# One attention, Fourier and FFN kernel: a list scheduler's order of operations replaced by a written one

## The chip, the cores and the metric

The kernel runs on one core of one Trainium2 chip. The metric is the device time of one execution in microseconds (us). Engines are named as the profile names them: PE (TensorE), PEld (its weight loads), DVE (VectorE), ACT (ScalarE), POOL (GpSimd), SP (SyncE, which issues most DMAs). PE is in order, as every engine is: an instruction that waits holds up all behind it on its engine.

## The reference

Sliding-window attention of 8 batches, 8 heads, 576 tokens and 64 columns a head, then the real part of a two-dimensional Fourier transform added to the input, a normalisation over the 512 columns, and a two-layer FFN with 2048 hidden columns:

```python
    mask = (rel >= 0) & (rel < window)          # window = 64
    scores = np.where(mask, scale * q @ k^T, -1e9)
    attn = np.exp(scores - max); attn = attn / (sum + 1e-09)
    x = (attn @ v), heads side by side           # 8 x 576 x 512
    X = np.fft.fft(np.fft.fft(x, axis=1), axis=2)
    u = x + np.real(X)
    un = (u - mu) / np.sqrt(var + 1e-06)
    out = u + np.maximum(un @ w_ch1, 0.0) @ w_ch2
```

## The kernel before

The 4608 tokens are 36 attention tiles of 128 rows (the code's T). Tiles 0 to 10 ("whole") work in f32 and are turned on PE; the others ("split") carry each number as a high and a low f16 half and are turned by transposing DMAs. For each tile: q and k are loaded, turned (flips, line 539; copies of the results, kst and qbd, by the helper `copy`, line 474 on ACT, 478 on DVE or GpSimd), multiplied (scores, 659 or 668 and 673), masked and exponentiated (ACT, 705), turned (722 on PE for whole tiles; for split ones the low half is a subtraction, `p_lo`, 736, and the turn a DMA, `p_turn`, 741), and multiplied with v (775). `v_own` (618) copies half a tile of v to the place from which the next tile reads it.

Eight Fourier stages, one a batch, follow the tiles (a radix-4 step on DVE at 810, its turn at 884 to 899, matmuls at 1035 to 1139). `norm_tile` gathers the mixed rows with an indirect DMA (GpSimd, 1246), takes the statistics (1261), scales (1295, un), and turns the result (1307, pu) into the operand of the FFN, uhl. The FFN works on 18 chunks of 256 tokens. Chunk 0 is in f32; chunks 1 to 10 use three f16 products (first layer 1507, ph; relu 1519 and 1522, hh; second layer 1487, po); chunks 11 to 17 use a seven-product scheme (`ffn7`: sums of operands at 1827, products px and py at 1755 and q at 1863, results gathered at 1896 to 1906, sent out at 1942 and 1945). The weights come in 32 pieces, which DVE converts (1394 to 1406) and ACT squares for their scale (1412).

All 3568 operations are first recorded: `op(eng, dur, prio, fn, reads, writes, ...)` keeps an engine, an assumed duration, a priority and, for 'alt' operations, a second engine that could do the same. Buffers are rings; a DMA, PE, DVE, ACT or POOL operation can take a slot once one is free. `Plan.order()` (278) then builds the program by a list scheduler: at each step it takes, among the ready operations, the one that can start first, with ties by priority; an operation that two engines can do goes to the one that would end sooner by a margin. Priorities come from formulas and from the tables NUDGE, LEAD and BIAS. DVE's operations that hold the port shared with GpSimd and GpSimd's own are assumed to exclude each other in time. The final loop (2021) emits the operations in that order; where the assumed gap on PE ahead of one is above 0.8 us, it puts in warm matmuls (1997), fillers that compute nothing, one for each 0.21 us beyond 0.4, in the early part only.

Of the kernel before, what the change touches and what calls it, by code (L numbers as in the profile page):

```python
# [67 lines left out]
NUDGE = {  # L68
    "": {0: 14.4, 1: 16.6, 2: -0.4, 3: 15.9, 4: 69.4, 5: 25.3, 6: -12, 8: 0.2, 10: 3.8, 11: -27.5},
    "even": {14: -0.3},  # L70
    "ffn7": {16: -0.6, 232: 0.3, 1276: 3.2, 2005: 0.6, 2006: 0.7, 2047: 12.4, 2100: -0.7, 2120: 1.3, 2141: -0.3, 2145: -0.1, 2146: 0.5, 2167: 0.2},
    "first": {21: 0.8, 32: -0.1, 62: 1.2},
    "odd": {34: -2.9},
    "piece": {0: 10.6},
    "split": {3: -0.1, 25: -0.2},
}
LEAD = {
    "": (
        0,
    ),  # L80
    "even": (
        0, 0, 0, 0, 0, 0, 0, 0,
    ),
    "ffn7": (
        0, 0, 0, 0, 0, 0, 0, 0, 0, 0, 0, 0, 0, 0, 0, 0,
        0, 0,
    ),
    "norm": (
        0, 0, 0, 0, 0, 0, 0, 0, 0, 0.4, 0, 0, 0, 0, 2.6, 2.6,
        3.9, 3.9, 3.9, 4, 3.9, 4.1, 3.9, 3.9, 3.9, 3.9, 3.9, 3.9, 3.9, 3.9, 3.9, 3.9,  # L90
        3.9, 3.9, 3.9, 3.9,
    ),
    "part": (
        0.3, 0.3, 0.3, 0.3, 0.3, 0.3, 0.3, 0.3, 0.3, 0.3, 0.3, 0.3, 0.3, 0.3, 0.3, 0.3,
        0.3, 0.3, 0.3, 0.3, -1.7, 0.3, 0.3, 0.3, 0.3, 0.3, 0.3, 0.3, 0.3, 0.3, 0.3, 0.3,
    ),
    "piece": (
        0, 0, 0, 0, 0, 0, 0, 0, 0, 0, 0, 0, 0, 0, 0, 0,
        0, 0, 0, 0, 0, 0, 0, 0, 0, 0.1, 0, 0.8, 0.8, 0.8, -9.9, -9.9,
    ),  # L100
    "pre1": (
        0, 0, 0, 0,
    ),
    "prep": (
        0, 0, 0, 0,
    ),
    "scale": (
        0, 0,
    ),
    "tail": (  # L110
        0, 0, 0, 0, 0, 0, 0, 0, 0, 0, 0, 0,
    ),
    "whole": (
        0, 0, 0, 0, -1.5, -1.5, -1.5, -1.5, -2.9, -2.9, -2.9, -2.9, -2.9, -2.9, -2.9, -2.9,
        -2.9, -2.9, -2.9, -2.9, -4.6, -2.9, -2.9, -2.9, -2.9, -2.9, -2.9, -2.9, -2.9, -2.9, -2.9, -2.9,
        -2.9, -2.9, -3.1, -3.1,
    ),
}
BIAS = {
    "ffn7": {21: -0.4},  # L120
    "first": {13: -0.8},
}
# [80 lines left out]
class Plan:  # L203
# [74 lines left out]
    def order(self):  # L278
# [5 lines left out]
        for o in self.ops:  # L284
            o.wait, o.ready = len(o.deps), 0.0
            for d in o.deps:
                d.outs.append(o)
# [1741 lines left out]
```

## Time and profile before

| | us |
|---|---|
| median of 3 runs (lowest, highest) | 946.46 (944.35, 946.49) |
| the profiled execution, its own time | 946.62 |
| its span | 944.8 |
| PE busy | 928.9 (98%) |
| DVE busy | 800.1 (85%) |
| ACT busy | 594.5 (63%) |
| POOL busy | 313.6 (33%) |

The span is the time between the first and the last instruction that the profile shows; 1.8 us lie outside it. Idle time of an engine that does not bound the kernel costs nothing by itself. What matters is where PE, busy 98% of the span, stands still, and what it waits for there.

### The profile page before, as it was taken

The numbers are of one execution on the slowest core, as the hardware profiler recorded it, in microseconds if no ns is written. First come the engines' busy times: TensorE is split into PE (matmuls) and PEld (weight loads), VectorE is DVE, ScalarE is ACT, GpSimd is POOL, SyncE is SP. The second block draws the span as 40 slices with busy tenths as digits, with TensorE's granted clock in tenths as the row PEclk, the third lists the DMA queues.
The fourth block names the chain that finished last, engine by engine and source line by source line (L and its number), as shares of the span: only waits on it lengthen the run. The fifth ranks groups of instructions, "written<-read, shape, count | busy, mean of one in ns | idle before, by whom it ended". The sixth has DMA issues, their size and how long they took to land.

```text
span 944.8 us, 25747 instructions
## 1 busy us (share of the span) xinstructions
PE 928.9 (98%) x10193; PEld 720.3 (76%) x10193; DVE 800.1 (85%) x1922; ACT 594.5 (63%) x1545; POOL 313.6 (33%) x348
## 2 busy tenths in 40 slices
PE   8999999999999999999999999999999999999997
PEld 6776767666676676677676667676788999999997
DVE  4989988888898798897788999799988788887776
ACT  6866587787686576878686675445346554655432
POOL 1111031242444453554342254313012255554120
PEclk9999999999999999999999999999999999999999
DMA  9979963279999999999999863513111343232000
GB/s 190 304 184 260 272 131 99 63 156 188 205 211 202 194 182 214 201 198 222 178 202 202 159 142 88 134 28 81 42 45 57 63 96 76 44 85 47 18 25 24
DMA packets 313257, 130.23 MB, mean 138 GB/s; under 512 B 291624, under 2 KB 292264, under 8 KB 313136
## 3 DMA queue, kind: packets, MB, share of 16 engines
q1 hardware_dynamic: 310272, 119.53, 59.1%
q0 software_dynamic: 2720, 8.92, 3.6%
q8 instruction: 80, 1.31, 0.6%
q14 instruction: 41, 0.34, 0.1%
q10 hardware_dynamic: 144, 0.13, 0.0%
HBM read 62.85 MB, written 22.04 MB: 90 GB/s over the span
## 4 chain that ended last, share of the span: by engine, by line
PE 75%; DVE 10%; DMA 6%; issue 5%; ACT 3%; POOL 1%; SPq 1%; POOLq 0%; ACTq 0%; DVEq 0%
PE ph L1507 19%; PE po L1487 19%; PE q L1863 11%; PE py L1755 5%; PE ph L1728 4%; PE px L1755 4%; PE pa L775 3%; PE pg L1043 2%; DMA pt<-flex 2%; PE psc L659 2%; PE pz L1095 2%; DMA mt<-md,gix 1%; DVE y L810 1%; PE pp L722 1%; ACT pr L705 1%
## 5 line engine op out<-in xcount | busy, mean ns | idle before, releaser
L1507 PE MATMUL ph<-uhl,w0s 128*128 128x256 f16 (+1 forms) x2040 | 262.1, 279 | 2.3 <-DVE hh L1522 1.3
L1487 PE MATMUL po<-w1s,hh 128*128 128x512 f16 (+1 forms) x1024 | 263.3, 393 | 0.6 <-DVE hh L1522 0.3
L1507 PEld LDWEIGHTS <-w0s 128*128 128x128 f16 x1920 | 185.6, 98 | 50.1 <-issue 3.0
L1487 PEld LDWEIGHTS <-hh 128*128 128x128 f16 x960 | 91.4, 98 | 82.3 <-DVE hh L1522 1.6
L1519 ACT ACTIVATE hh<-ph 128x512 f16<-128x512 f32 x80 | 47.3, 592 | 56.3 <-PE ph L1507 50.9
L705 ACT ACTIVATE pr<-pr,nm 128x128 f32<-128x128 f32 x200 | 77.5, 391 | 1.9 <-DVE nm L694 1.8
L1246 POOL DMA_INDIRECT mt<-md,gix x34 | 42.8, 1259 | 87.4 <-DVE xu L1261 39.8
L1863 PEld LDWEIGHTS <-qbd 128*128 128x128 f16 x672 | 64.9, 98 | 7.6 <-DVE qbd L1827 0.5
L1522 DVE SCALAR_TENSOR_TENSOR hh<-ph,hh 128x512 f16<-128x512 f32 x80 | 54.7, 684 | 16.3 <-ACT hh L1519 15.8
L1863 PEld LDWEIGHTS <-kst 128*128 128x128 f16 x504 | 49.3, 98 | 5.7
L478 POOL COPY yp<-y 128x1024 uint16<-128x1024 uint16 x24 | 28.7, 1195 | 73.4 <-DVE y L810 52.2
L1827 DVE TENSOR_TENSOR flex<-flex 128x256 f32<-128x256 f32 x91 | 40.2, 442 | 14.8 <-ACT flex L1822 6.0
L694 DVE CUSTOM_DVE_ANT_0 pr<-psc,mskb 128x128 f32<-128x128 f32 x200 | 45.5, 282 | 0.6 <-PE psc L659 0.5
L1755 PEld LDWEIGHTS <-wa 128*128 128x128 f16 x750 | 45.6, 98 | 0.2
L1755 PEld LDWEIGHTS <-w0s 128*128 128x128 f16 x720 | 44.9, 98 | 0.2
L1798 ACT ACTIVATE flex<-flex 128x384 f32<-128x384 f32 x40 | 20.7, 518 | 37.2 <-DVE flex L1778 37.1
L1840 ACT CAST qbd<-flex 128x1024 f16<-128x1024 f32 x28 | 29.2, 1042 | 23.7 <-DVE flex L1827 12.9
L1728 PE MATMUL ph<-uhl,w0s 128*128 128x256 f16 x384 | 43.5, 273 | 0.0
L474 ACT COPY qbd<-qbd 64x1024 uint16<-64x1024 uint16 x40 | 41.7, 1043 | 2.7 <-DMA qbd<-flex 1.7
L478 POOL COPY yT<-py 128x1024 uint16<-128x1024 uint16 (+2 forms) x24 | 26.5, 1107 | 47.7 <-DMA py<-yp 45.0
L1863 PE MATMUL q<-w1s,qbd 128*128 128x256 f16 x336 | 41.4, 273 | 0.2 <-DVE qbd L1827 0.2
L1728 PEld LDWEIGHTS <-w0s 128*128 128x128 f16 x384 | 37.6, 98 | 5.2
(285 smaller groups left out, 2132.9 us busy)
## 6 DMA issues: line engine op xcount, KB each, us to landing
wd<-in_moe_w_ch SPq DMA_DIRECT2D x26, 512.0 KB, 5.5
out<-xu SPq DMA_DIRECT2D x34, 256.0 KB, 2.8
kn<-in_k SPq DMA_DIRECT2D x32, 256.0 KB, 3.4
qn<-in_q SPq DMA_DIRECT2D x32, 256.0 KB, 4.5
xd<-xa SPq DMA_DIRECT2D x30, 256.0 KB, 3.1
xu<-xd SPq DMA_DIRECT2D x30, 256.0 KB, 3.5
flex<-in_v SPq DMA_DIRECT2D x22, 256.0 KB, 3.8
md<-mp SPq DMA_DIRECT2D x24, 192.0 KB, 3.5
```

The costliest lines, as they stand in the source:

```text
L474: nc.scalar.mul(out, in_, scale) if scale is not None else nc.scalar.copy(out, in_)
L478: eng.tensor_copy(out, in_)
L694: nc.vector.tensor_tensor_reduce(out=t["pr", jj][:, hp], in0=t["ps", jj][:, hp], in1=mskb[:, m : m + P], scale=-0.125, scalar=3.0e38, op0= ...
L705: nc.scalar.activation(pr, src, AF.Exp, bias=t["nm", jj][:, hp : hp + 1], scale=-1.0, accum_out=t["rc"][:, hp, jj])
L1246: nc.gpsimd.indirect_dma_start(out=mts[T], out_offset=None, in_=mds[pb][0 : HR if n < 4 else 2 * HR], in_offset=bass.IndirectOffsetOnAxis( ...
L1487: nc.tensor.matmul(t["po"][i], l_, r_, start=(f == 0 and x == 0), stop=(f == NKF - 1 and x == len(mm) - 1))
L1507: nc.tensor.matmul(ph, l_, r_, start=(x == 0), stop=(x == len(mm) - 1))
L1519: nc.scalar.activation(t["hh", pr][:, 0], ph, AF.Relu)
L1522: nc.vector.scalar_tensor_tensor(out=hh[:, 1], in0=ph, scalar=0.0, in1=hh[:, 0], op0=ALU.max, op1=ALU.subtract)
L1728: nc.tensor.matmul(ph, l_, r_, start=(x == 0), stop=(x == len(mm) - 1))
L1755: nc.tensor.matmul(to[:, x], l_(a, k_), r_(b_, k_), start=(y == 0), stop=(y == 5))
L1863: nc.tensor.matmul(t["q"][q_][:, y], l_[:, a, i, m], r_(b_, m), start=(s_ + y + m + x == 0), stop=(s_ == 3 and m == 1 and x == 2 and (y == ...
```

## The change

The list scheduler is gone. A tuple ORDER of 3568 numbers holds the order of all operations on all engines: a number n at or above 0 is operation n on its first engine, and -1 - n is operation n on its second. `Plan.follow(ORDER)` walks it, sets engine and place, and works out assumed starts only to find the gaps on PE in which warm matmuls go. The tables NUDGE, LEAD and BIAS are removed. The operations, their arithmetic and their buffers' rings are the same; code behind the tables stands 30 lines lower. The tuple was made by a search with a price on the waits of GpSimd for the shared port, over five sets of assumed durations.

```diff
-NUDGE = {
-    "": {0: 14.4, 1: 16.6, 2: -0.4, 3: 15.9, 4: 69.4, 5: 25.3, 6: -12, 8: 0.2, 10: 3.8, 11: -27.5},
...
+ORDER = (
+    2, 3, 0, 1, 174, 178, 179, 173, 176, 177, 4, 181, 186, 196, 182, 199, 197, 201, -203, 200, 204, 183, 184, 187,
...
-    def order(self):
+    def follow(self, order):
...
+        for n in order:
+            o = self.ops[max(n, -1 - n)]
+            o.eng = list(o.durs)[n < 0]
+            o.dur, o.ready = o.durs[o.eng], 0.0
+            for d in o.deps:
+                late = self.LATE[d.eng] * (o.slack if "PE" in o.durs else 0.0 if d.eng in o.durs else o.wary)
+                o.ready = max(o.ready, d.free + (self.SEM if d.eng not in o.durs or d.lat else self.SELF)[d.eng] + late)
+            locks = o.lock if o.eng == "POOL" else o.eng == "DVE" and o.port
+            st = max(free[o.eng], o.ready, port if locks else 0.0)
+            for b in o.allocs:
+                st = max(st, slots[b.ring].pop(0))
+            gap, o.st = st - free[o.eng], st
...
-        for o, gap in zip(plan.order(), plan.gaps):
+        for o, gap in plan.follow(ORDER):
```

Operations on each engine, before and after: PE 726 and 726, DVE 1265 and 1231, ACT 847 and 807, POOL 262 and 336, DMAs 468 and 468. Warm matmuls: 49 and 32. Three places follow, as the built program has them, in the engine's order; names are those of tiles with a running number, and x4 is four alike.

PE ahead of the first bank (ph) of the FFN's chunk 0: turns of probabilities (pp), of k and q (pk, pq) and of the normalised tiles (pu). Before:

```order
L539 MATMUL pk_1154<-ident,kn_1111 128x128 x4
L1307 MATMUL pu_1165<-ident,un_1085 128x128 x4
L1997 LDWEIGHTS ident
L1997 MATMUL warm<-ident 128x256
...
L722 MATMUL pp_0_1178<-ident,flex 128x128 x4
L1307 MATMUL pu_1187<-ident,un_1113 128x128 x4
L722 MATMUL pp_1_1195<-ident,flex 128x128 x4
L539 MATMUL pq_1202<-ident,qn_1134 128x128 x4
L1507 MATMUL ph_0_1211<-uhl_1166,w0s 128x256 x4
```

The same place on PE after, up to the masks of a later tile's scores (psc):

```order
L1169 MATMUL pm_1026<-mp_0_983,put 128x512
L569 MATMUL pq_1067<-ident,qn_943 128x128 x4
L752 MATMUL pp_0_1075<-ident,flex 128x128 x4
L569 MATMUL pq_1081<-ident,qn_963 128x128 x4
L1337 MATMUL pu_1098<-ident,un_1096 128x128 x4
L752 MATMUL pp_0_1112<-ident,pr_0_821 128x128 x4
L698 LDWEIGHTS ident
L698 MATMUL psc_0_1121<-mskb,ident 128x512
```

Of the turns ahead of chunk 0, the first pu now stands between a pq and a pp, with the scores (psc) of a later tile behind, and the warm matmuls between them are gone.

ACT ahead of the second copy of uhl (the operand of chunk 0). Before:

```order
L1412 ACTIVATE junk_6_1024,ssq_86<-w0s 128x512
L474 COPY v_81<-v_82 64x1024
L474 COPY kst<-pk_1053 128x512
L474 ACTIVATE qbd_78<-pq_1068 128x512
L474 COPY kst<-pk_1080 128x512
L474 COPY yT_910<-py_1129 128x4x128
L705 ACTIVATE flex,rc_1145<-psc_0_1089,nm_0_1124 128x128 x4
L705 ACTIVATE flex,rc_1145<-psc_1_1091,nm_1_1141 128x128 x4
L474 COPY uhl_1166<-pu_1165 128x4x128
L474 COPY flex<-pp_0_1178 128x512
L474 COPY uhl_1166<-pu_1187 128x4x128
```

The same place on ACT after:

```order
L1442 ACTIVATE junk_3_1030,ssq_87<-w1s 128x512
L1442 ACTIVATE junk_7_1032,ssq_86<-w0s 128x512
L735 ACTIVATE flex,rc_1036<-psc_0_994,nm_0_1034 128x128 x4
L504 COPY pt_1_1042<-pp_1_1041 128x512
L735 ACTIVATE flex,rc_1036<-psc_1_996,nm_1_1060 128x128 x4
L504 COPY kst<-pk_1053 128x512
L504 ACTIVATE qbd_78<-pq_1067 128x512
L504 COPY flex<-pp_0_1075 128x512
L504 ACTIVATE qbd_77<-pq_1081 128x512
L504 COPY uhl_1099<-pu_1098 128x4x128
L504 COPY pt_0_1113<-pp_0_1112 128x512
L504 COPY uhl_1099<-pu_1146 128x4x128
```

The copy of v and one copy of yT that stood here are gone from ACT; copies of pt, kst and qbd stand ahead of the uhl copies.

GpSimd at the end of its list: sums of operands and low halves (1827, in the new file 1857) and the additions of results (1896, now 1926). Before:

```order
L1205 TENSOR_TENSOR up_3_13890<-t_17_13663,up_3_13890 128x256
L1827 TENSOR_TENSOR flex<-flex 128x256
L1827 TENSOR_TENSOR kst<-flex,kst 128x768
L1827 TENSOR_TENSOR flex<-flex 128x256 x4
L1896 TENSOR_TENSOR xu_12625<-xu_12625,flex 128x256
L1827 TENSOR_TENSOR qbd_77<-flex,qbd_77 128x1024
L1827 TENSOR_TENSOR flex<-flex 128x256
L1896 TENSOR_TENSOR xu_13364<-xu_13364,flex 128x256 x2
```

The end of GpSimd's list after:

```order
L1926 TENSOR_TENSOR xu_12648<-xu_12648,flex 128x256
L1926 TENSOR_TENSOR xu_12884<-xu_12884,flex 128x256 x2
L1857 TENSOR_TENSOR kst<-flex,kst 128x768
L1857 TENSOR_TENSOR flex<-flex 128x256 x2
L1857 TENSOR_TENSOR kst<-flex,kst 128x768
L1857 TENSOR_TENSOR flex<-flex 128x256 x2
L1857 TENSOR_TENSOR qbd_77<-flex,qbd_77 128x1024
L1857 TENSOR_TENSOR kst<-flex,kst 128x768
L1857 TENSOR_TENSOR flex<-flex 128x256
L1926 TENSOR_TENSOR xu_13333<-xu_13333,flex 128x256 x2
```

More low halves of kst stand on GpSimd now in the last chunk (three, before one), ahead of the same two final additions.

## Rows read from the trace of the kernel before

**Rows 1.** Stretches: us, then PE, PEld, DVE, ACT, POOL busy, PEclk, DMA, GB/s

```profile
0.00:6.00 6.00, 3.91 (x19) 2.79 (x20) 0.00 (x0) 1.28 (x1) 2.66 (x12) 1.00 0.69 155
6.00:42.00 36.00, 34.69 (x502) 28.40 (x501) 27.17 (x52) 27.82 (x100) 3.10 (x4) 1.00 0.95 253
42.00:47.00 5.00, 3.89 (x54) 2.86 (x52) 4.81 (x12) 4.73 (x24) 1.53 (x1) 1.00 0.93 316
47.00:73.00 26.00, 25.88 (x236) 18.88 (x235) 22.92 (x54) 15.72 (x58) 3.95 (x6) 1.00 0.77 194
73.00:84.00 11.00, 9.09 (x89) 6.69 (x88) 10.62 (x25) 8.07 (x27) 2.03 (x2) 1.00 0.97 229
...
100.00:675.00 575.00, 570.51 (x5927) 403.51 (x5926) 502.79 (x1295) 393.26 (x1030) 210.85 (x226) 1.00 0.79 161
675.00:940.00 265.00, 264.77 (x3235) 245.60 (x3232) 215.99 (x459) 133.33 (x277) 87.29 (x96) 1.00 0.22 52
...
sum 945.00, PE 928.91 PEld 720.27 DVE 800.09 ACT 594.51 POOL 313.62; mean PE 103.21 PEld 80.03 DVE 88.90 ACT 66.06 POOL 34.85
```

**Rows 2.** The same for the warm matmuls alone, 0 to 100 us

```profile
73.00:84.00 11.00, 1.75 (x10) 1.00 0.97 229
...
sum 100.00, PE 9.34; mean PE 1.56
```

**Rows 3.** Chain that ended last, 67 to 84 us: start, length, what

```profile
74.99 0.46 DVE un L1295
...
78.89 1.97 ACT flex L705 x11
```

**Rows 4.** PE timeline, 71 to 84: start, length, what, idle before

```profile
79.51 0.66 PE L1307 MATMUL pu<-ident,un 128*128 128x128 f32 x4 [0.75 <-ACT flex L705]
...
81.40 0.64 PE L1307 MATMUL pu<-ident,un 128*128 128x128 f32 x4
...
83.22 1.25 PE L1507 MATMUL ph<-uhl,w0s 128*128 128x256 f32 x5
```

**Rows 5.** ACT by line and form, 0 to 84: busy, mean ns, idle

```profile
L474 ACT COPY v<-v 64x1024 uint16<-64x1024 uint16 x5 | 5.2, 1043 | 2.5 <-issue 2.5
...
L474 ACT COPY pt<-pp 128x512 f32<-128x512 f32 x6 | 3.6, 612 | 3.3 <-PE pp L722 3.3
```

**Rows 6.** Waits of PE, 100 to 675 us: total, times, longest

```profile
PE pa L775 <- DMA pt<-flex: 0.9, 2, 0.6
```

**Rows 7.** Timeline of PE around attention tile 21

```profile
350.24 0.64 PE L659 MATMUL psc<-kst,qbd 128*64 128x128 f16 x16
...
361.65 1.47 PE L1507 MATMUL ph<-uhl,w0s 128*128 128x256 f16 x12
362.96 1.46 PE L1487 MATMUL po<-w1s,hh 128*128 128x512 f16 x6
...
367.50 0.85 PE L775 MATMUL pa<-v,pt 128*64 128x64 f16 x42 [0.26 <-DMA pt<-flex]
```

**Rows 8.** Timeline of SP's DMA queue, 359 to 366 us

```profile
361.00 4.17 SPq L741 DMA_TRANSPOSE pt<-flex  x2
```

**Rows 9.** Line 741, transposes of probabilities, 330 to 690: min/median/max

```profile
L741 SPq DMA_TRANSPOSE pt<-flex x34: 1231/1288/2818, 333.3 to 593.6; - x34
...
DMA to landing us min/median/max: 3.1/4.8/6.6
```

**Rows 10.** Groups of POOL and of DVE by line and form, whole span

```profile
L736 POOL TENSOR_TENSOR flex<-pr,flex 128x512 f16<-128x512 f32 x20 | 26.8, 1342 | 24.4 <-ACT flex L474 19.0 <-DVE flex L478 5.0 <-DMA pt<-flex 0.4
...
L736 DVE TENSOR_TENSOR flex<-pr,flex 128x512 f16<-128x512 f32 x30 | 21.4, 715 | 0.7 <-ACT flex L474 0.4
```

**Rows 11.** Timelines of PE, POOL and DVE, end of the span

```profile
939.35 0.82 PE L1863 MATMUL q<-v,qbd 128*128 128x256 f16 x6
...
939.78 1.41 POOL L1896 TENSOR_TENSOR xu<-xu,flex 128x256 f32<-128x256 f32 x2 [24.58 <-DVE flex L1906]
...
941.22 0.48 DVE L1898 SCALAR_TENSOR_TENSOR xu<-q,osc,xu 128x256 f32<-128x256 f32 x1 [0.20 <-POOL xu L1896]
```

More of the change, by code (lines that the diff above doesn't have):

```diff
@@ L67 @@
 C_AT = ("fh", "fh", "pt", "pt")
-NUDGE = {
-    "": {0: 14.4, 1: 16.6, 2: -0.4, 3: 15.9, 4: 69.4, 5: 25.3, 6: -12, 8: 0.2, 10: 3.8, 11: -27.5},
[L70 to L122, printed above, removed]
+ORDER = (
[149 rows of a table added]
+)
 VS = 64.0
@@ L199 @@
 class Op:
-    __slots__ = ("eng", "dur", "lat", "fn", "deps", "outs", "prio", "wait", "ready", "allocs", "bufs", "idx", "durs", "margin", "port", "slack", "wary", "group", "lock")
+    __slots__ = ("eng", "dur", "lat", "fn", "deps", "outs", "prio", "wait", "ready", "allocs", "bufs", "idx", "durs", "margin", "port", "slack", "wary", "group", "lock", "free", "st")
 class Plan:
@@ L217, in __init__ @@
     def __init__(self, rings, fifo):
[L218 removed]
+        self.rings, self.fifo, self.ops = dict(rings), fifo, []
         self.slack = self.wary = 0.0
@@ L276, in pe_time @@
         return t
[L278 removed]
+    def follow(self, order):
         busy = {}
[L280 to L282 removed]
+        free = {e: 0.0 for o in self.ops for e in o.durs}
         slots = {r: [0.0] * n for r, n in self.rings.items()}
[L284 to L287, printed above, removed]
[L288 to L298 removed]
@@ L352, in order @@
             free[o.eng] = end
-            if o.lock if o.eng == "POOL" else o.eng == "DVE" and o.port:
+            if locks:
                 port = end
-            done = end + o.lat
-            for b in o.allocs:
-                s_ = sorted(slots[b.ring])
-                slots[b.ring] = s_[1:]
-                if b.ring in line:
-                    line[b.ring].pop()
+            o.free = end + o.lat
             for b in o.bufs:
                 b.left -= 1
-                b.free_at = max(b.free_at, done + self.SEM[o.eng])
+                b.free_at = max(b.free_at, o.free + self.SEM[o.eng])
                 if b.ring and b.left == 0:
                     slots[b.ring].append(b.free_at)
-            for x in o.outs:
-                x.wait -= 1
-                late = self.LATE[o.eng] * (x.slack if "PE" in x.durs else 0.0 if o.eng in x.durs else x.wary)
-                x.ready = max(x.ready, done + (self.SEM if o.eng not in x.durs or o.lat else self.SELF)[o.eng] + late)
-                if not x.wait:
-                    for e in x.durs:
-                        avail[e].append(x)
-            res.append((st, o))
+            res.append((o, gap))
         self.span = max(free.values())
-        self.times = [st for st, _ in res]
-        return [o for _, o in res]
+        return res
 @with_exitstack
```

65 lines of the change are left out of this document (1 added, 64 removed), and 148 rows, old and new, of the table ORDER.

## The prediction

> **What bounds the kernel now.** I read the busy time of each engine over the whole span first, then the same by stretches, then the waits of TensorE and the chain of work in the stretches where it stands still. The sum at the foot of the windows [rows 1] has PE busy 928.91 us of a span of 944.8: TensorE is the bound almost everywhere, and its granted clock is at the full level (1.00, that is 2.4 GHz) in every stretch that matters. The change keeps every matmul of the work, so it can only return time in which PE does nothing useful. That time is idle time plus the warm matmuls (fillers that compute nothing). Before 84 us the stretches leave PE idle for 2.09 + 1.31 + 1.11 + 0.12 + 1.91 = 6.54 us [rows 1], and the warm matmuls add 9.34 [rows 2]: 15.9 us. The long middle (100 to 675 us) leaves 575 - 570.51 = 4.49, the last third (675 to 940) 0.23 [rows 1], and from the last matmul, which starts its last group at 939.35 [rows 11] and ends near 940.1, to the end of the span it is 4.7. Together some 25 us, 2.7% of the span: that is all that any order of the same work could win, and the head holds more than half of it.
>
> **The head, 0 to 84 us.** The first FFN chunk needs two normalised tiles, turned by PE (line 1307, pu), copied by ACT (474, uhl). Here the chain of waits [rows 3] shows the second normalised tile written by DVE from 74.99 on for 0.46 us, so it was there at 75.45. Yet PE turns the first tile at 79.51, the second at 81.40, and starts the chunk at 83.22 [rows 4]. What lay between is ACT's queue: the chain has eleven instructions of exponentials on ACT for 1.97 us at its end [rows 3], and the copies and flips stand behind them. In 73 to 84 us PE lost 11 - 9.09 = 1.91 idle [rows 1] and 1.75 to warm matmuls [rows 2], 3.66 us.
>
> What the new order does there: (1) The five copies of v on ACT in this stretch (64x1024, 5.2 us [rows 5]) leave ACT; six such moves in the head go to GpSimd. In exchange ACT gets two more copies each of kst, qbd and pt, one more square, and two fewer of yT, so five more of some 0.6 us (0.612 for pt [rows 5]; the others are of the same size), 3.0 us. Ahead of the second copy of uhl ACT so has 5.2 - 3.0 = 2.2 us less to do. (2) PE's queue: the two flips pu now stand between other flips, with the scores and the probabilities-times-v of a later attention tile between the second one and the chunk, and no warm matmul ahead of it; before there were ten in three groups. The useful PE work ahead of the chunk's first bank is about the same in both orders. (3) Warm matmuls of the head go from 49 to 32: two fewer at the start, five fewer near 42 to 47 us, ten fewer in 73 to 80. (4) DVE's queue ahead of the second normalised tile grows by 0.5 us, summed from the mean times of the operations that now stand there; the 5.9 us for which that tile lay ready [rows 3, 4] cover that.
>
> If ACT's queue alone sets the head, it gains 2.2. If the gaps go where the warm matmuls go, it gains the 3.66 of 73 to 84 us, plus seven warm matmuls elsewhere of 9.34 / 49 = 0.19 [rows 2], 1.3: 5.0. It is no loss by these rows: ACT, whose queue held the flips, has less ahead of them, and DVE's extra half microsecond lies under 5.9. I take the middle, **-3.6**. What hides the rest: nothing is waiting behind the chunk's start, since PE was idle or busy with fillers; from 84 us on PE is full (16 of 16 us in the trace), so each microsecond won there moves everything after it.
>
> **The middle, 84 to 675 us.** Attention tiles, Fourier stages and norms run beside ten FFN chunks. PE lost 4.49 us in many small waits, two of which, 0.9 us, were for the transposed probabilities pt [rows 6]. The new order shuffles every engine's list here: in attention, Fourier and norm steps 24 operations fewer on ACT, 8 more on DVE and 16 more on GpSimd. The distance on PE between a tile's scores and its product with v was 24.2 us of PE work in the median tile and falls to 23.1. What counts are the shortest. In tile 21 the second score ran at 350.24 for 0.64 and ended near 350.81 by its pitch; the product waited for pt until 367.50 [rows 7], a chain of 16.7 us. In the new order three tiles allow less than that: tile 35 has eight FFN steps of 1.31 (361.65 to 362.96 [rows 7]) and some 1.5 us of other work between, about 12.0 us; two others 15.1 and 15.5. If their chains take what that of tile 21 took, PE waits 4.7 + 1.6 + 1.2 = 7.5 us more. But tile 21's chain was held up on the DMA queue: the first of its two transposes was issued at 361.00, and the pair took 4.17 us [rows 8] where one takes 1.29 in the median [rows 9]; with the second at once behind the first and the shortest landing (3.1 us [rows 9]) the chain is 10.2 + 1.3 + 3.1 = 14.6, and only tile 35 waits, 2.6 us. The other end is that all 4.49 us of waits go. So the middle lies between -4.5 and +7.5. I take **0**: half of the old waits gone (-2.2) and tile 35 late by 2.6, by the row of the shortest landing rather than tile 21's own, because behind the last attention tile no further tile's loads and transposes are queued.
>
> **GpSimd's load.** Net 74 operations go to GpSimd (262 to 336), among them the subtraction that leaves the low half of the probabilities: 1.34 us there and 0.72 on DVE [rows 10]. Work off PE costs nothing while PE has its inputs: in 675 to 940 us, where 38 of them go, PE was idle for 0.23 us with DVE busy 216 of 265 and GpSimd 87 [rows 1]. I cost it at 0 with ends 0 and the +7.5 above, of which a slow GpSimd step would be part, because it stands in that chain. The Trainium skill, GPSIMD Engine Reference, section 4.1 Engine selection, gives two-input elementwise work to VectorE and calls GpSimd about twice as slow; the trace agrees (1.34 against 0.72). Its section 1 (Specifications) adds that the two share SBUF interfaces and contend; going by that alone, the moves would stretch steps on both engines, and the sum would come out at the late end of the middle, 949.8, where the idle row above leaves it at 942.2.
>
> **The end.** The last chunk closes four output banks, six matmuls a group, a group each 0.65 us. Before, the last four groups were those of the banks 0, 1, 2, 3. Now the last but one group of bank 3, which stood ahead of these, stands between bank 2's last and bank 3's last, so that banks 0, 1 and 2 are complete one group sooner. The chain after the last group's start (939.35) goes over GpSimd's two additions of the second tile (939.78, 1.41 us), which rest on bank 1, to DVE's last step at 941.22 [rows 11] and the output DMA. One group sooner on bank 1 takes at most 0.65 off it; DVE's step on bank 3 then follows the last matmul as before. I take **-0.6** (ends 0 and -0.65).
>
> **Sum.** Against the profiled execution (946.62, its span 944.8 and 1.8 outside): 946.6 - 3.6 + 0 - 0.6 = 942.4. The median of the runs is 946.46, 0.16 lower; so 942.2.
>
> **Rivals.** *Late probabilities.* The three short tiles take the chain of tile 21: +7.5 in the middle. With the head's 2.2 and nothing at the end the time is 946.5 - 2.2 + 7.5 = 951.8; with the head's 3.6 and the end's 0.6 it is 949.8. The sign turns once the waits added in the middle exceed the 4.2 won outside it, and the kernel is measurably slower from about 7. For it: two tiles did wait for pt before. Against: tile 35 is the last one. *The head does not move.* DVE was busy 10.62 of 11 us in 73 to 84 [rows 1]. If it, with half a microsecond more ahead of the second normalised tile and the weights' conversions beside it, is what the first chunk really waits for, the idle time stays as longer waits without fillers: 946.5 - 0.6 = 945.9, no change. Against: that tile lay ready for 5.9 us. *Everything closes.* All waits of the middle go and the head gives 5.0: 946.5 - 5.0 - 4.5 - 0.6 = 936.4. *The clock drops where fillers are gone.* In 73 to 84 us useful PE work is 9.09 - 1.75 = 7.34 us; at the lower level (1.2 GHz) it takes 7.3 us more, and the time is 942.2 + 7.3 = 949.5. Against: in 47 to 73 us there is no warm matmul, and the clock is 1.00 with PE busy 25.88 of 26 [rows 1]; it needs the gaps to stay after the fillers have left. The Trainium skill, TensorE: Matmul & The Clock Gate, Part 1, says that an engine that has been idle is granted half its clock; no stretch of this trace shows that.
>
> **How the numbers follow.** Forecast (head won, middle about level) 0.50; everything closes 0.08; head does not move, or the middle eats what the head gives, 0.27; late probabilities 0.10; clock 0.05. A measurement of this kernel tells apart about 0.3%, 2.8 us. Below 943.6 lie the forecast and the closing case: faster 0.58. Between 943.6 and 949.3: 0.27. Above: 0.15. The range goes from 936.5, at the closing case, to 949.8, which takes in the late probabilities with the head won: 1 in 10 is left above, and less below.
>
> **What would show it.** Right: the first FFN bank starts 2.2 to 5.0 us earlier than 83.22, PE in the stretch before it has no idle time longer than a few tenths, and the rest of the trace is the same work shifted; the wait for pt at tile 35 is below 3 us; the last matmul ends about 4.1 us before the end of the span. Wrong: the idle time of 100 to 675 us is over 8 us with pt as its releaser, or waits for GpSimd's low halves appear in 675 to 940 us, or a granted clock below 1.00 ahead of the first chunk.

## The result, and the profile after

The changed kernel takes 953.3 us (median of 6 runs, 949.79 to 953.92) against 946.48 beside it (6 runs, 943.87 to 950.62): a ratio of 1.0065, 95% interval 1.0038 to 1.0093. It is slower by 0.65%, where 942.2 us was forecast. Its profiled execution took 953.54 us, with a span of 951.8.

The first view is the one of [rows 1]: busy time by stretch of the changed kernel (from:to, length, then PE, PEld, DVE, ACT, POOL busy with their counts, granted clock, DMA share, GB/s).

```profile
73.00:84.00 11.00, 11.00 (x120) 9.49 (x118) 10.66 (x22) 8.18 (x32) 1.29 (x2) 1.00 0.84 212
100.00:675.00 575.00, 564.05 (x5857) 395.31 (x5856) 504.11 (x1275) 372.18 (x1005) 234.33 (x255) 1.00 0.77 159
675.00:940.00 265.00, 263.92 (x3210) 243.36 (x3209) 204.33 (x431) 130.34 (x271) 125.94 (x138) 1.00 0.23 54
```

In 73 to 84 us PE was busy for 9.09 of 11 before, and is now busy throughout. In the middle it stands idle for 575 - 564.05 = 10.95 us, where it was 4.49 [rows 1]. The head, as PE's timeline has it (start, length, line, what, for [rows 4]):

```profile
73.94 0.60 PE L1337 MATMUL pu<-ident,un 128*128 128x128 f32 x4
...
76.37 0.66 PE L1337 MATMUL pu<-ident,un 128*128 128x128 f32 x4
76.96 1.15 PE L805 MATMUL pa<-v,pt 128*64 128x64 f32 x32
78.04 4.15 PE L1537 MATMUL ph<-uhl,w0s 128*128 128x256 f32 x18
```

The first FFN bank starts at 78.04 instead of 83.22 [rows 4], 5.2 us earlier. To see where that went, I laid the two traces side by side by the same amount of useful matmul work done (a mark of work lies at a later time on the clock than its number), and read off how much later or earlier the changed kernel stands there. Such a reading moves by 1 to 2 us with the placing of the marks: -4.8 us at 100 us of work, -4.1 at 240, +0.6 at 300, +2.2 at 340, +0.4 at 360, +3.5 at 420, +7.5 at 440, +6.3 at 660, +7.6 at 920. So two stretches cost it: 240 to 340 of work (the losses lie at 290 to 350 us on the clock of the trace) and 380 to 440 (400 to 460 us). PE's waits in 100 to 675 us (waiting instruction, what it waited for: total, times, longest), the view of [rows 6]:

```profile
PE ph L1537 <- DMA uhl<-up: 3.5, 1, 3.5
PE ph L1537 <- DVE hh L1552: 3.4, 2, 2.4
PE po L1517 <- DVE hh L1552: 2.2, 3, 1.1
PE pa L805 <- POOL v L508: 0.5, 1, 0.5
PE pz L1125 <- DVE g L506: 0.5, 1, 0.5
PE pz L1125 <- DVE g L1083: 0.5, 1, 0.5
```

There is no wait for pt at all. What is late is the FFN's own input: uhl, which is the longest single wait and comes by a DMA, hh (its low half, written by DVE), and the Fourier stage's g, mostly DVE's results. The longest wait for DVE is at 457.80, and the granted clock falls behind it (windows of 10 us):

```profile
440.00:450.00 10.00, 9.96 (x134) 6.69 (x133) 9.54 (x16) 6.08 (x17) 5.79 (x7) 1.00 0.70 145
450.00:460.00 10.00, 7.65 (x91) 5.26 (x89) 9.69 (x31) 5.51 (x19) 5.98 (x8) 0.90 1.05 184
460.00:470.00 10.00, 10.00 (x96) 6.06 (x95) 7.18 (x19) 6.87 (x15) 4.13 (x4) 0.93 0.96 173
```

And the end, timelines of PE, GpSimd and DVE (for [rows 11]):

```profile
946.92 0.82 PE L1893 MATMUL q<-v,qbd 128*128 128x256 f16 x6
...
946.71 1.41 POOL L1926 TENSOR_TENSOR xu<-xu,flex 128x256 f32<-128x256 f32 x2 [7.70 <-DVE flex L1936]
...
947.84 0.88 DVE L1928 SCALAR_TENSOR_TENSOR xu<-q,osc,xu 128x256 f32<-128x256 f32 x2 [0.30 <-PE q L1893]
```

From the start of the last group to the end of the span it is 951.8 - 946.92 = 4.9 us, where it was 944.8 - 939.35 = 5.4.

The line that explains the longest of the waits for DVE stands in DVE's timeline, ahead of the wait of 457.80:

```profile
440.36 0.69 DVE L1552 SCALAR_TENSOR_TENSOR hh<-ph,hh 128x512 f16<-128x512 f32 x1 [1.53 <-ACT hh L1549]
440.97 4.38 DVE L766 TENSOR_TENSOR flex<-pr,flex 128x512 f16<-128x512 f32 x1
445.28 0.68 DVE L815 TENSOR_TENSOR xa<-pa,rc 128x512 f32<-128x512 f32 x1
...
457.06 0.68 DVE L1552 SCALAR_TENSOR_TENSOR hh<-ph,hh 128x512 f16<-128x512 f32 x1
```

One subtraction (p_lo) takes 4.38 us, where the same step takes 0.69. DVE has no idle time from there to 457.06, so the 3.7 us are still missing when it writes hh. GpSimd in the same microseconds:

```profile
440.46 1.08 POOL L1276 DMA_INDIRECT mt<-md,gix  x1 [0.16 <-issue]
441.55 1.15 POOL L508 COPY yT<-py 128x1024 uint16<-128x1024 uint16 x1
442.68 1.15 POOL L595 TENSOR_TENSOR flex<-qn,flex 128x512 f16<-128x512 f32 x1
443.77 1.03 POOL L508 COPY v<-v 64x1024 uint16<-64x1024 uint16 x1
```

GpSimd runs a row of steps without a gap until 444.80, and p_lo ends 0.55 us behind the row, at 445.35. I did not see this at first. It took most of the experiments to come to it; they are told by the question that each was to answer, nearly in the order in which they ran.

### The profile page after: what moved, and what is told of

Read it like the earlier page. It is cut to its first block, busy times and chain, and to the rows that moved or that the text cites. A ratio compares the mean times of both kernels' runs of the same rounds, so it can differ in the third digit from the quotient of the medians.

```text
span 951.8 us, 25801 instructions
## 1 busy us (share of the span) xinstructions
PE 930.3 (98%) x10176; PEld 720.5 (76%) x10176; DVE 798.1 (84%) x1880; ACT 575.7 (60%) x1547; POOL 384.0 (40%) x430
## 4 chain that ended last, share of the span: by engine, by line
PE 74%; DVE 13%; DMA 4%; ACT 4%; issue 3%; POOL 1%; SPq 0%; DVEq 0%; POOLq 0%; ACTq 0%
PE ph L1537 19%; PE po L1517 18%; PE q L1893 12%; PE ph L1758 4%; PE py L1785 4%; PE px L1785 3%; PE pz L1125 2%; PE psc L689 2%; PE pa L805 2%; PE pg L1073 2%; DMA uhl<-up 1%; ACT pr L735 1%; DMA py<-yp 1%; DVE y L840 1%; DVE hh L1552 1%
## 5 line engine op out<-in xcount | busy, mean ns | idle before, releaser
L508 POOL COPY v<-v 64x1024 uint16<-64x1024 uint16 x27 | 30.3, 1123 | 75.8 <-DMA v<-in_v 35.9
L508 POOL COPY yp<-y 128x1024 uint16<-128x1024 uint16 x19 | 21.0, 1103 | 57.9 <-DMA uhl<-up 29.1
L1857 POOL TENSOR_TENSOR flex<-flex 128x256 f32<-128x256 f32 x42 | 30.7, 730 | 33.0 <-DVE flex L1857 22.5
L1857 DVE TENSOR_TENSOR flex<-flex 128x256 f32<-128x256 f32 x70 | 31.5, 450 | 12.5 <-POOL flex L1857 6.5
L1785 PE MATMUL py<-uhl,wa 128*128 128x128 f16 x570 | 41.3, 219 | 0.0
```

Source lines behind the costliest of these rows:

```text
L508: eng.tensor_copy(out, in_)
L1785: nc.tensor.matmul(to[:, x], l_(a, k_), r_(b_, k_), start=(y == 0), stop=(y == 5))
L1857: return lambda eng=nc.vector: eng.tensor_tensor(out=o, in0=a, in1=b, op=al)
```

## The experiments

A number in the tuple ORDER names an operation, so the diffs of orders show one line of many. Every ratio is to the kernel before, run on the same chip.

### Which part of the order costs

**e1_head**: the changed kernel's first 763 operations (to some 195 us), and then all others as the kernel before had them. **e2_mid**: the changed kernel with the operations of some 195 to 525 us as before. The first line that e2 takes out of the changed kernel's ORDER:

```diff
@@ -98,70 +98,70 @@
-    2212, 2214, 460, 628, 2213, 785, 621, 622, 2216, 636, 2215, -727, 461, -624, -728, 629, 462, 2217, -464, 464, 624, 780, 630, 2220,
...
```

> The new order for the first 763 operations (to about 195 us, the whole head), then all the others in the old order and on their old engines. By work done on TensorE the new kernel is 4.8 us ahead at 100 us and 11 us of loss come between 280 and 510 us. If the loss belongs to the order of the middle, whatever its mechanism, the head's gain is kept: 941.5 to 943. If the head's gain is only an earlier start that the middle cannot use (its inputs come no sooner), the old middle loses it too: 945 to 947.

> The new order, but with the operations that run from about 195 to 525 us in the old order and on their old engines (the head and everything from 525 us on as in the new kernel). If the loss is made in that stretch: 953.3 less 11, 941 to 943.5. If the last stretches of the new order cost by themselves, 945 or more; if the loss follows the head's earlier start, 950 or more.

Measured: e1 940.07 us, ratio 0.9933 (0.9915 to 0.9951); e2 939.77, 0.9942 (0.9921 to 0.9964). Both beat both kernels, and both by more than was expected of them. So the new head is worth some 6 us (the intervals go from 3 to 8), the new last third costs nothing that can be told from e1, and the loss lies in the order of 195 to 525 us.

**e5_late_mid** (new head, the old order to 366 us, the new one for 366 to 525, the old one behind) and **e13_from_313** (new head, the old order for 195 to 313 us, the new one from there). The first line that e5 takes out:

```diff
@@ -98,35 +98,35 @@
-    2212, 2214, 460, 628, 2213, 785, 621, 622, 2216, 636, 2215, -727, 461, -624, -728, 629, 462, 2217, -464, 464, 624, 780, 630, 2220,
...
```

> New head, old order to about 366 us, new order from there to about 525 us, old order to the end: the later half of the disputed stretch alone. By work done, the new kernel lost about 3.5 us between 280 and 340 us of work and about 6 to 7 between 360 and 450. If losses belong to places in the order: 940.1 + 6 = 944.5 to 948. If the later half only loses because the earlier half left it late: 940 to 942.

> The new head, the old order from 195 to 313 us, the new order from there to the end. If the loss starts at the late v and uhl near 300 us and the rest of the new middle only suffers from starting late: 941 to 944. If each part of the new middle loses by itself: 947 to 951 (11 less the 5.3 that are lost between 280 and 340 us of work).

Measured: e5 950.14, 1.0058 (1.0038 to 1.0078); e13 950.15, 1.0042 (1.0021 to 1.0063). In 380 to 440 us of work e5 loses 4.6 us and e13 4.9, against 1.1 before and 8.6 in the changed kernel (7 with the marks placed a little otherwise). Either part of the new middle loses by itself, and the losses do not add: by the ratios e5 lies 11.8 us above e1 and e13 10.3, where the whole new middle costs 12.5. e5 came out above both of its forecasts. Part of both losses is a wait for hh behind 530 us, 4.38 us at 533.86 in e5 and 2.37 us at 542.07 in e13, a place to which e18 comes back.

### Which engine does what

**e3_engines**: the new order with 108 operations of 266 to 525 us back on the engines that they had before. **e4_engines_rev**: the old order with these 108 on their new engines. One line of e3:

```diff
-    2531, 1728, 2532, 1980, -1778, 1981, 1930, 1920, 1982, 1921, 1756, 1758, 1925, 1931, 1932, 1571, 1759, -1761, 1761, 2012, 2540, 2533, 1945, 2541,
+    2531, 1728, 2532, -1981, -1778, -1982, 1930, 1920, 1982, 1921, 1756, 1758, 1925, 1931, 1932, 1571, 1759, -1761, 1761, 2012, 2540, 2533, 1945, 2541,
```

> The new order kept, but the 108 operations between about 266 and 525 us that changed their engine go back to their old engine, at their place in the order. Port theory (GpSimd's extra steps there stretch DVE's: 8 us more of stretching on DVE between 300 and 520 us than before): 944 to 948. Queue theory (late inputs ahead of FFN steps in the queues, whoever does them): 951 to 954.

> The counterpart: the old order kept, and the same 108 operations put on the engines that the new order gives them. Port theory: 951 to 955. Queue theory: 946 to 948.

Measured: e3 962.82, 1.0186 (1.0162 to 1.0211); e4 964.33, 1.018 (1.0152 to 1.0208). Both are far worse than either theory had them: an order fits its own engines, and neither half can be exchanged alone. The two say nothing on the cause.

### Is it GpSimd's load on the shared port?

**e6_pool_tt** adds to e1 20 times three two-input products on GpSimd in 290 to 520 us, **e7_pool_ms** 20 times five memsets at the same places.

```diff
+    nc_spare = {864, 1037, 1183, 1222, 1235, 1237, 1303, 1404, 1428, 1455, 1489, 1496, 1498, 1530, 1532, 1680, 1729, 1748, 1768, 1916}
...
+            if o.idx in nc_spare:
+                for _ in range(3):
+                    nc.gpsimd.tensor_tensor(out=unit, in0=unit, in1=unit, op=ALU.mult)
```

> New head and old middle (the kernel of 940.1), and on GpSimd, at 20 places between 295 and 515 us where it stood idle for over 2 us, three extra 128x128 two-input multiplications of a constant by itself that nobody reads there (about 1.2 us a place, 24 us in all, more than the 14 by which the new order loads GpSimd there). Port theory: DVE is stretched by 7 us or more between 290 and 520 us (16.0 in the kernel it is built on, 23.3 in the new one), and the time goes to 945 or more. Queue theory: stretched or not, the old order has the room, 940 to 942.

> The same 20 places with five writes of a constant (memset 128x128, about 1 us a place), which read nothing. Both theories: 940 to 941.5, little stretching on DVE, if the stretching needs GpSimd's operand reads; if any GpSimd work stretches DVE or delays GpSimd's own queue, as much as in the run with the multiplications.

Measured: e6 941.52, 0.9963 (0.9951 to 0.9976); e7 941.76, 0.9955 (0.9939 to 0.9971), 1.5 and 1.7 us behind e1 by the medians, 2.8 and 2.1 by the ratios, with intervals that touch or overlap that of e1. The group of GpSimd steps that was added, in 290 to 520 us (busy, mean ns | idle before), of e6 and then of e7:

```profile
L2035 POOL TENSOR_TENSOR unit<-unit 128x128 f32<-128x128 f32 x60 | 32.6, 544 | 3.1
```

```profile
L2035 POOL MEMSET unit<- 128x128 f32 x100 | 21.8, 218 | 4.6
```

DVE's steps of 290 to 520 us were stretched beyond their usual lengths by 23.5 us in all in e6, 16.5 in e7, 16.0 in e1 and 23.3 in the changed kernel. As e6 had the same sum as the changed kernel and lost little, I dropped the port as the cause. That was too quick: a sum does not say where the stretch falls. In e6 no single step was stretched by as much as 1 us, though the added steps stand in rows of three.

### Single waits, taken one by one

**e8_v_behind** moves the split of v behind norm 9's scale on ACT, ahead of the wait for uhl; **e10_norm10** moves norm 10's small steps ahead of a blocked copy on GpSimd; **e11_both** does both; **e9_hh_first** moves DVE's step on hh up by up to three places.

```diff
-    1155, 862, 2320, 1209, 863, 864, 1238, 2316, 2317, 1190, 1030, 2319, 1160, 1191, 1181, 1182, 2321, 2324, 872, 865, 866, 2325, 880, -868,
+    1155, 862, 2320, 1209, 863, 864, 1238, 2316, 2317, 1190, 1030, 2319, 1160, 1191, 2321, 2324, 872, 865, 866, 2325, 880, -868, 1181, 1182,
```

```diff
-    868, 2322, -1215, 2323, 1032, 965, -1035, 1035, 1278, 1161, 1244, 873, 874, -1246, -1242, 881, 2326, 1184, 1185, 1186, 1192, 1242, 1033, 2327,
+    868, 2322, -1215, 2323, 1032, 965, -1035, 1278, 1161, 1244, 873, 874, 875, 1035, -1246, -1242, 881, 2326, 1184, 1185, 1186, 1192, 1242, 1033,
```

```diff
-    1024, 1025, 1026, 1175, 843, -845, 853, 2301, 2299, -1178, 1178, 2303, 2306, 1016, 1023, 845, 854, 2304, 2305, 997, -1028, -1029, 1273, 855,
+    1024, 2299, 1025, 1026, 1175, 843, -845, 853, 2301, -1178, 1178, 2303, 2306, 1016, 1023, 845, 854, 2304, 2305, 997, -1028, -1029, 1273, 855,
```

The first pair of lines is of e8, the second of e10, the third of e9; e11 has the first two.

> The new order with one swap: the two steps that scale tile 19's v (ACT, then DVE) stand behind norm tile 9's last scaling and splitting, as in the old order, not ahead of them. In the trace of the new kernel ACT waited 2.28 us at 299.1 for the load of v with the norm's scaling behind it, and TensorE 3.65 us at 305 for the operand uhl that follows. Queue theory: that wait of TensorE falls from 3.65 to about 1.6 us and what follows shrinks with it, 949.5 to 952. If uhl is late for another reason (its transposing DMA landed 7.64 us after its issue): 952 to 954.

> The new order with another swap: on GpSimd norm tile 10's three small steps stand ahead of the copy yp of tile 17, not two steps behind it. That copy waited 6.9 us for a buffer that the transposing DMA of uhl still read, so norm 10's steps ran at 312.3 though their inputs were there at 304.0, and ACT stood still for 5.27 us behind them. Queue theory: ACT's 5.27 go, TensorE's losses between 313 and 350 us (about 3) halve: 950.5 to 952.5. If these losses come from DVE alone: 952.5 to 954.

> Both swaps. If the losses of 300 to 350 us come from these two places: 948 to 950.5, near the sum of the two. If every wait that goes is replaced by the next: 951 to 954.

> The new order, but on DVE 28 of the 52 low-half steps of the FFN's relu (line 1552 of the new file) in the disputed stretch stand up to three DVE operations earlier, as far as their own inputs allow. Queue theory: TensorE's waits for these (5.6 us in 100 to 675 us) go in good part: 948 to 950.5. Port theory: the steps ahead of them are stretched all the same, but these are no longer behind them, so about as much; only if the waits are replaced by others of the same length (late inputs of attention steps): 952 to 955.

Measured: e8 949.49, 1.0039 (1.0022 to 1.0056); e10 951.29, 1.0067 (1.0042 to 1.0091); e11 951.08, 1.0051 (1.003 to 1.0072); e9 956.95, 1.0132 (1.0105 to 1.016). In e8 the wait for uhl only fell from 3.5 to 3.1, since the transposing DMA took 8.05 us there; e8 is the only one of the four below the changed kernel's 1.0065 by more than 2 us, and the intervals overlap. In e9 other waits took the place of those for hh (po for hh 4.5 us in five, pz for g 3.4 in four). None of the four meets the loss in 380 to 440 us of work, which stayed at 4.9 in e8, e10 and e11, and at 5.9 in e9.

### Is it DVE's load?

**e15_dve_load** adds nine times three two-input products on DVE to e1, in 402 to 464 us. **e14_dve_back** gives nine steps of 404 to 476 us of the changed kernel back from DVE to ACT, **e16_pool_back** four copies back from GpSimd to ACT, **e17_all_back** all 13.

```diff
+            if o.idx in extra:
+                for _ in range(3):
+                    nc.vector.tensor_tensor(out=unit, in0=unit, in1=unit, op=ALU.mult)
```

The first lines are of e15, the next of e14 (1448 in place of -1449), the last of e16; e17 has both of the last two.

```diff
-    -1303, 1303, 2414, 1442, 2415, 1326, 1327, 1628, 1443, 1304, 1447, 1453, 2417, 1444, -1317, 2419, 1317, 1467, 1312, -1449, 1305, -1450, 2422, 1631,
+    -1303, 1303, 2414, 1442, 2415, 1326, 1327, 1628, 1443, 1304, 1447, 1453, 2417, 1444, -1317, 2419, 1317, 1467, 1312, 1448, 1305, -1450, 2422, 1631,
```

```diff
-    1671, -1735, 2467, 2471, 1641, 2469, 1647, 1654, 1705, 1673, 1674, 2472, 1676, 1677, 2474, 2475, 1348, 2473, 1530, 1678, 1682, -1680, 1680, 1683,
+    1671, -1735, 2467, 2471, -1642, 2469, 1647, 1654, 1705, 1673, 1674, 2472, 1676, 1677, 2474, 2475, 1348, 2473, 1530, 1678, 1682, -1680, 1680, 1683,
```

> New head and old middle (the kernel of 940.1), with three extra 128x128 multiplications on DVE that nobody reads at 9 places between 402 and 464 us, 0.3 us each, 8 us in all: as much as the new order adds to DVE's busy time between 380 and 440 us of TensorE's work. Load theory: TensorE loses 3 to 5 us more there, 943 to 945.5. Order theory: the old order has room for it, 940 to 941.5.

> The new order, with the nine steps that went from ACT to DVE between 404 and 476 us back on ACT, at their place in the order (about 4.5 us less on DVE, ACT has 26 us to spare there). Load theory: the loss there falls from 8.6 (4.9 without the drop of the clock) to 2 or 3, 948.5 to 951. Order theory: 952 to 955.

> The new order, with the four copies that went from ACT to GpSimd between 404 and 476 us (three of v, one of yT) back on ACT. If these copies stretch DVE's steps there (the subtraction of the low half took 1.38 us in the mean against 0.68): DVE's busy time there falls by 2 to 4 us, 949.5 to 951.5. If not: 952 to 955.

> Both: all thirteen steps back on ACT. Load theory: DVE's busy time between 380 and 440 us of TensorE's work near the old 50.5, the loss there near 1.5, 947 to 949.5. Order theory: the loss there stays at 4 or more, 951 to 955.

Measured: e15 946.57, 0.9983 (0.995 to 1.0016), 6.5 us above e1 by the medians and 4.7 by the ratios: DVE's time is scarce there. But e14 took 953.12, 1.0069 (1.0037 to 1.0101), e16 951.88, 1.0068 (1.004 to 1.0095), and e17 952.06, 1.0062 (1.0034 to 1.009). DVE's busy time in that stretch was back at the old level in e17 (51.9 us against 50.5) and the loss was still 6.8 us. So the load that the new order adds there is not the cause. The reason was in e17's trace, here DVE and then GpSimd:

```profile
442.37 2.36 DVE L766 TENSOR_TENSOR flex<-pr,flex 128x512 f16<-128x512 f32 x1
...
441.90 1.15 POOL L508 COPY yT<-py 128x1024 uint16<-128x1024 uint16 x1
443.01 1.15 POOL L595 TENSOR_TENSOR flex<-qn,flex 128x512 f16<-128x512 f32 x1
```

The copy of v is gone from GpSimd here, its row ends at 443.01 + 1.15 = 444.16, and p_lo ends 0.57 us behind it, at 444.73. In the changed kernel the row ended at 444.80 and p_lo 0.55 behind it. p_lo took 3.35 us in e14, 3.42 in e16 and 4.40 in e5: all of them still had it. Two more such places lie ahead of lost time: y at 341.60 (3.90 us, for some 1.3) ahead of g and of PE's waits at 347, and xu at 392.61 (3.28, for some 1.5), which left DVE late ahead of the wait at 412. The first of them in the changed kernel, DVE and then GpSimd:

```profile
341.60 1.71 DVE L840 TENSOR_TENSOR y<-xa 128x256 f32<-128x256 f32 x2
343.23 2.26 DVE L840 TENSOR_TENSOR y<-y 128x128 f32<-128x128 f32 x2
...
342.99 1.19 POOL L1011 TENSOR_TENSOR f<-f,xe 128x388 f32<-128x388 f32 x1
344.14 1.21 POOL L766 TENSOR_TENSOR flex<-pr,flex 128x512 f16<-128x512 f32 x1
```

Here the row does not hold DVE to its end. Each of the short steps of y and of xu that was stretched ended 0.02 to 0.55 us behind the end of one GpSimd step, and the next DVE step came in between. Why p_lo had to let two or three of GpSimd's steps pass in every one of these runs, and y and xu one at a time, was not found out. In the old middle, in e1 and e2, at most one operation of 290 to 520 us is stretched by more than 1.4 us; in the changed kernel five are.

### GpSimd made to take its turn

**e18_turns** leaves the order of each engine as it is. At the three places GpSimd waits, five times in all, for the DVE step to which the order gives the turn.

```diff
+    turns = {1169: 1200, 1101: 1106, 1430: 1523, 1703: 1672, 1512: 1123}
+    turn, seen = (cp.tile([P, 8], F32, name=n) for n in ("turn", "seen"))
+    flag = {d: (turn[:, k:k + 1], seen[:, k:k + 1]) for k, d in enumerate(turns.values())}
...
+            if o.idx in turns:
+                nc.gpsimd.tensor_copy(out=flag[turns[o.idx]][1], in_=flag[turns[o.idx]][0])
...
+            if o.idx in flag:
+                nc.vector.memset(flag[o.idx][0], 1.0)
```

> The changed kernel with five turns at the shared port enforced: at 341, 392 and 441 us GpSimd waits for the DVE step that the plan places ahead of it. After that DVE step a memset of one column is added on DVE, and ahead of the GpSimd step a copy of that column on GpSimd, so that it waits (two yT copies also move behind their DVE steps, the copy of v behind the low half of norm 16). What is computed is the same. In the changed kernel DVE's steps there were held while GpSimd ran a row of steps without a gap: y at 341.60 took 3.90 us, xu at 392.61 took 3.28, p_lo at 440.97 took 4.38 where 0.69 is usual, and DVE was late by 1.7, 1.8 and 3.6 us behind them, ahead of PE's waits of 346, 410 and 454 us. Theory A (rows of GpSimd steps, its copies among them, hold up DVE at single places, and that is what PE waits for): the three steps fall to about 1.5, 1.5 and 0.8 us, PE's waits at 344 to 347 (1.4 us lost), 410 (1.4) and 454 (2.5, and 1.7 of lower clock behind it) go for the most part; ratio 0.9985 to 1.001 instead of 1.0065, the time near 946 to 947. Theory B (the places of the FFN's steps in the queues are wrong whatever their lengths are, as the runs with DVE's and GpSimd's load taken back would have it): the stretches go, but other waits come in their place, since GpSimd is now 1 to 2 us later; ratio 1.004 to 1.008, loss in 380 to 440 us of work still above 4.5.

Measured: 945.34, 0.9995 (0.9976 to 1.0014), 0.7% or 6.6 us better than the changed kernel (3.5 to 9.8 by the two intervals), by five waits, as theory A had it. DVE and GpSimd at the first and the third place:

```profile
341.23 0.75 DVE L843 TENSOR_TENSOR y<-xa 128x256 f32<-128x256 f32 x2
341.90 0.61 DVE L843 TENSOR_TENSOR y<-y 128x128 f32<-128x128 f32 x2
...
342.60 0.19 POOL L2032 COPY seen<-turn 128x1 f32<-128x1 f32 x1 [6.31 <-DVE turn L2038]
...
437.51 0.68 DVE L769 TENSOR_TENSOR flex<-pr,flex 128x512 f16<-128x512 f32 x1
```

The steps are back at 1.3 and 0.68 us. PE's waits of 347, 412 and 457.80 us are gone: from 340 to 440 us of work the kernel loses 0.2 us more than before does, where the changed kernel lost 5.3 more. What took their place stands behind 530 us: DVE's hh late again, with a wait of 2.26 us at 541.49 and a lower clock behind it.

```profile
530.00:540.00 10.00, 9.23 (x126) 5.84 (x125) 9.70 (x15) 3.29 (x5) 5.14 (x4) 1.00 0.83 171
540.00:550.00 10.00, 8.51 (x50) 5.39 (x50) 8.21 (x22) 4.71 (x15) 2.56 (x5) 0.83 1.06 153
```

```profile
541.49 1.66 PE L1540 MATMUL ph<-uhl,w0s 128*128 128x256 f16 x12 [2.26 <-DVE hh L1555]
542.95 2.77 PE L1520 MATMUL po<-w1s,hh 128*128 128x512 f16 x6
```

This execution took 949.43 us, 4.1 above the median of its twelve (942.28 to 950.02). The wait is not its own: the traces of e13, e14 and e17 have one of 2.37, 2.27 and 2.39 us for hh between 542 and 548 us, with no lower clock behind it.

**e19_more_turns** adds three turns in that place.

```diff
-    turns = {1169: 1200, 1101: 1106, 1430: 1523, 1703: 1672, 1512: 1123}
+    turns = {1169: 1200, 1101: 1106, 1430: 1523, 1703: 1672, 1512: 1123, 2018: 1927, 1800: 1794, 1922: 1955}
```

> The kernel of e18_turns with three more turns of the same kind, between 531 and 540 us: GpSimd's low half of q waits for DVE's low halves of the probabilities (531.13, 3.08 us for two where 1.4 is usual), its part xe for DVE's y (537.41, 1.99 for 0.61), and its copy of v for DVE's low half of v (539.32, 1.52 for 0.69). In e18_turns DVE came 3 us late out of these, PE waited 2.26 us for hh at 541.49, and the granted clock was 0.83 in 540 to 550. What is computed is the same. Theory A (single held DVE steps are what PE waits for): that wait goes, and with it the lower clock behind it, 3.2 us together; ratio 0.995 to 0.998 to the kernel before. Theory C (rows of GpSimd steps only move on and hold another DVE step that is as tight): a wait of 1 us or more turns up elsewhere after 530 us, and the ratio stays at 0.998 to 1.001.

Measured: 943.43, 0.9976 (0.9958 to 0.9994): now faster than before, by little. Against e18 it is 1.8 us by the ratios, where theory A had 3.2, and the two intervals overlap; that the wait and the lower clock are gone, the trace shows. The same windows and PE's waits of 100 to 675 us:

```profile
530.00:540.00 10.00, 10.00 (x135) 6.69 (x134) 8.78 (x28) 4.94 (x13) 5.33 (x7) 1.00 0.93 183
540.00:550.00 10.00, 10.00 (x109) 6.56 (x108) 9.87 (x24) 5.25 (x13) 6.09 (x9) 1.00 0.95 180
```

```profile
PE ph L1540 <- DMA uhl<-up: 3.5, 1, 3.5
PE ph L1540 <- DVE hh L1555: 1.2, 2, 1.0
...
PE po L1520 <- DVE hh L1555: 0.5, 1, 0.5
```

The waits for hh that were 3.4 and 2.2 us in the changed kernel are 1.2 and 0.5 here. Eight waits on GpSimd, and nothing moved on any engine, return 8.4 us (1.0065 - 0.9976, of 946). With the held steps back at their usual length and PE's waits behind them gone, that shows the cause of the loss behind 330 us. (Waits at places where no step was held were not tried, so what a later GpSimd does by itself has no run of its own.) What stays open is the wait for uhl, which all of these kernels keep. Its chain in the changed kernel:

```profile
293.29 5.74 DMA flex<-in_v
...
301.84 7.64 DMA uhl<-up
```

ACT stood 2.28 us for v's load in front of norm 9's scale, and the transposing DMA took 7.64 us from its issue. Before, PE started that chunk at 309.48, 5.96 us after DVE had written `up` (303.52); here it is 309.53 and 301.82, 7.7 us. Why the transpose is slower here was not found out; moving v's split (e8) was not enough. Between 240 and 320 us of work e19 loses 5.4 us more than the kernel before (from -4.3 to +1.1), e1 only 1.4: most of what keeps e19 behind e1 (4.1 us by the ratios) lies around this wait.

## Why the prediction was wrong

**What bounds the kernel**: right. PE is busy for 98% in both, and each microsecond of the difference is time in which PE stands still or runs at the lower clock.

**The head** (-3.6, ends 2.2 and 5.0): right in mechanism, low in size. The first bank came 5.2 us earlier, PE has no idle time in 73 to 84 us and no warm matmul, and over the same work the gain at 100 us is 4.8. e1, which keeps the head alone, gains 6.3 by its ratio (4.6 to 8.0). So the gaps went where the fillers went; the end of 5.0 was the better reading than the middle of the two.

**The middle** (0, ends -4.5 and +7.5): wrong, in size and in mechanism. Over the same work the changed kernel goes from -4.8 to +6.3 between 100 and 660 us, 11.1 us. I looked for the loss at pt, since PE had waited for it before [rows 6] and three tiles had less room [rows 7 to 9]. No wait for pt is left, and tile 35 has none. Of the signs that the prediction named, the idle time over 8 us came, but not with pt as its releaser; waits for GpSimd's low halves in 675 to 940 us did not (PE waited there 0.7 us for DVE and 0.4 for ACT).

**GpSimd's load** (0): this is the step that failed. I took its price from 675 to 940 us, where PE was idle for 0.23 us [rows 1]. That stretch is another stage, in which neither order leaves PE waiting for long: it is idle for 0.23 us before and 1.08 now, with GpSimd busy for 87 and 126 us. In 290 to 520 us DVE's steps that have both inputs in SBUF stand in one queue with hh and g, for which PE comes soon, and there GpSimd's steps hold them up. The 1.34 and 0.72 us of [rows 10] told how long a step takes on either engine, not what it does to the other. e6 shows that it was not the amount either: 32.6 us of added work cost 1.5 to 2.8. What costs is a row of GpSimd steps without a gap on top of a DVE step ahead of a tight input. In place of the 0, three such places, with the lower clock behind one of them, cost 6.6 of the 11 us (e18); most of the rest stands around the wait for uhl, whose cause is open.

The rows of DVE that tell which steps are held (minimum, median and longest in ns, in 290 to 520 us of the changed kernel):

```profile
L766 DVE TENSOR_TENSOR flex<-pr,flex x14: 683/692/4385, 295.3 to 498.6; 128x512 f16<-128x512 f32 x14
...
L1552 DVE SCALAR_TENSOR_TENSOR hh<-ph,hh x33: 678/684/692, 291.1 to 517.0; 128x512 f16<-128x512 f32 x33
```

p_lo, with two inputs from SBUF, goes up to 4.4 us. hh, which reads PSUM, never takes more than 0.692, though GpSimd is busy for 113.7 of these 230 us. The Trainium skill, GPSIMD Engine Reference, section 1 (Specifications), says just that: the contention is with DVE instructions that have two SBUF inputs or run in a two-port mode. The prediction drew on that section and gave 949.8 by it, and then let a row of another stage overrule it. The trace agrees with the page; that p_lo let three GpSimd steps pass, one behind the other, is only in the trace.

Why the new order does this, although it was searched with a price on that port, can in part be read in the code; no run tested it by a change of the planner. The planner lets GpSimd's and DVE's steps exclude each other only where both are marked as holding the port. The copies of v (line 638 before, 668 after) are put down with `lock=False`, as are those of yp, and the new order gives GpSimd more copies of v (9 in 290 to 520 us; e1 has 3). On the chip the copies of v and yT were in the row that held p_lo, though in e17, without the copy of v, p_lo was still held, for 2.36 us. And the planner lets the two take turns as written, while nothing on the chip makes GpSimd wait: e18 is what it takes.

**The end** (-0.6): right, 5.4 to 4.9 us from the last group's start.

**The rivals.** Late probabilities had a time near the result (949.8 to 951.8) by a mechanism that did not occur. The head did move. The lower clock did come, but behind one of PE's long waits of the middle, and not in the head. The chance of 0.15 for slower was too small because all of it hung on pt and the clock; that GpSimd holds DVE was given a time (949.8) and no chance, though the change sends GpSimd 74 more operations.

**The range** (936.5 to 949.8) missed 953.3 for the same reason: its upper end held 7.5 us in the middle, for late probabilities with a slow GpSimd step as part of them, where the middle lost 11.1, and nothing for the wait for uhl.

## What to carry to other kernels

Where two engines share a port, price moved work by where it lands, and not by its sum: look in the trace for single steps several times their usual length, and at what the other engine ran in that time. A row from another stage says little about this one; take the price of a load from the stretch where it goes. And an order written out holds only what is synchronised: where it relies on engines taking turns, a small wait that enforces the turn can be worth more than the order itself. The best kernel here is the new head with the old middle, 940 us.
